# Two small transfers of an attention and phase-mixing kernel move from SyncE's queue to ScalarE's, and the first K follows the first Q directly

## The chip, the cores and the metric

The kernel runs on one core of a Trainium2 chip. The core has five engines with queues of their own: TensorE (PE, matrix products), VectorE (DVE), ScalarE (ACT), GpSimd (POOL) and SyncE (SP), which here does nothing but issue transfers. Transfers are carried out by 16 DMA engines that all queues share. The metric is the time of one execution on the device in microseconds; lower is better. The kernel before takes 221.73 us (median of three runs, 221.65 to 223.01).

## The reference

An attention block with polynomial features is followed by a token-mixing block whose input is the attention's output. Sizes: batch 4, 4 heads, 1088 tokens, head size 32, sketch size R = 8; the second block works on 128 columns.

```python
def phi(x):                                    # 32 -> 8 * 8 features
    a = einsum('rd,bhsd->bhsr', S1, x)
    b = einsum('rd,bhsd->bhsr', S2, x)
    return einsum('bhsi,bhsj->bhsij', a, b).reshape(..., 64)

q_p, k_p = phi(q), phi(k)
kv  = einsum('bhsf,bhsd->bhfd', k_p, v);  z = sum(k_p, axis=2)
num = einsum('bhsf,bhfd->bhsd', q_p, kv)
den = einsum('bhsf,bhf->bhs', q_p, z) + 1e-06
x   = (num / den), heads side by side          # (4, 1088, 128)

theta = x @ w_theta
yr = einsum('ts,bsd->btd', w_tok_r, x * cos(theta))
yi = einsum('ts,bsd->btd', w_tok_i, x * sin(theta))
u  = x + yr + yi
out = u + maximum(u @ w_ch, 0)
```

The weights and the sketch matrices S1, S2 come as 64-bit floating-point numbers, q, k and v as 32-bit ones.

## The kernel before

The kernel is written as a list of operations (`op`), each with its engine, the buffers that it reads and writes, and a function that emits its instructions. They are not emitted in the order of the text: `SEQUENCE` (L51) is a list of operation numbers written out by hand, and `Layout.issue` walks it. Each engine gets its instructions in that order and works them off strictly in that order; between engines there are semaphore waits where one reads what another wrote. `PLACES` gives each buffer a fixed slot in the on-chip memory.

`FILLS` (L127) adds empty matrix products (`spin`, L388) on TensorE in front of chosen operations: `(290, 1)` means one in front of operation 290. A positive count writes to a bank that nobody reads. A negative count, which the list of before doesn't use, writes into the bank that the operation itself is about to fill, for each new bank tile of that operation.

The work has three stages.

- Loading and features (about the first 57 us). For each of the four batches Q, K and V are loaded as 128 partitions by 1152 numbers (576 KB each, L661; some K a second time, L699). ScalarE squares a whole tensor and sums it (Q in L979, K in L683) so that a scale can be chosen; VectorE rounds the tensor to a half-precision part (`hf`, L338) and a rest; TensorE multiplies the parts (L354) and turns blocks (L1003 for Q, L780 for K). GpSimd issues accumulating transfers (L348) that add a rounded part to a second copy.
- The sketch matrices. S1 and S2 arrive in a small tile `st` by two transfers: L404 (`s_t`, 128 rows of 16 numbers, the matrix repeated for the four heads) and L405 (`s_2`, 8 rows of 32 numbers). Both write a tile that VectorE has cleared first (L411). `L418` on ScalarE is the first reader; it turns the 64-bit words into 32-bit numbers together with VectorE (L338, L341) and L430. The largest entry (`m2`, L460) goes over TensorE (L441) to a scale (L472), and the scaled matrices (L473, L474) feed the small products `psc`, `sbt`, `sbk` of GpSimd that the feature products need.
- Token mixing (the rest). The rows of the two 1088 x 1088 weight matrices are loaded (L614) and unpacked by ScalarE (L619, L621), and TensorE forms the products with a scheme that shares blocks between batches.

The order around the change, by engine, at the start. SyncE issues: Q of batch 0 (L661); the two small transfers (L404, L405); K of batches 0 to 3; Q of batches 1 and 2; the first rows of the token weights; and so on. ScalarE: the load of its function tables and a warm-up with the sine (L394), then L418, the square of Q0 (L979), of K0 (L683), L430, the square of K1, a scale of Q0 (L993), the square of K2, and L472 to L474. TensorE: 12 empty products, the turns of Q0, L441, a sum over partitions (`sm`,`ones`), 15 empty products (operation 64, which is one itself, and its fill of 14), and then the products of K0's rounded part (`hf`).

The planner's dependency rule is in `Layout.op`: each operation of ScalarE is made to depend on the first one (`leader`), the warm-up behind the table load. It adds edges to the planner's graph; the order that is emitted is the written list.

Of the kernel before, what the change touches and what calls it, by code (L numbers as in the profile page):

```python
# [48 lines left out]
QFIX = 2.006  # L49
NFIX = 1.002  # L50
SEQUENCE = (  # L51
# [74 lines left out]
)  # L126
FILLS = (  # L127
    (290, 1), (64, 14),
)


# [15 lines left out]
class Layout:  # L147
# [12 lines left out]
    def op(self, eng, dur, fn, w=(), r=(), acc=(), hold=(), lk=0, kind=0, mode=0, n=1, fly=0.0):  # L160
        o = Op()
        o.lk, o.fly, o.stage, o.kind, o.mode, o.n = lk, fly, self.stage, kind, mode, n
        o.i, o.eng, o.dur, o.fn = len(self.ops), eng, dur, fn
        o.succ, pred, o.bufs = [], set(), []
        if eng == "A":
            pred.update(self.leader)
            self.leader = self.leader or [o.i]

        def parts(x):
            return x if isinstance(x, tuple) else (x, None)  # L170

        def hits(table, b, key):
            t = table.get(b, {})
            return [v for k, v in t.items() if k is None or key is None or k == key or (
                isinstance(k, tuple) and k[0] == key) or (isinstance(key, tuple) and key[0] == k)]

        for x in r:
            b, key = parts(x)
            pred.update(hits(self.last_w, b, key))
            for s in hits(self.sums, b, key):  # L180
                pred.update(s)
            o.bufs.append(b)
        for x in list(w) + list(acc):
            b, key = parts(x)
            pred.update(hits(self.last_w, b, key))
            for s in hits(self.readers, b, key):
                pred.update(s)
            o.bufs.append(b)
        for x in w:
            b, key = parts(x)  # L190
            for s in hits(self.sums, b, key):
                pred.update(s)
        for x in r:
            b, key = parts(x)
            self.readers.setdefault(b, {}).setdefault(key, set()).add(o.i)
        for x in w:
            b, key = parts(x)
            if key is None:
                self.last_w[b] = {None: o.i}
                self.readers[b], self.sums[b] = {}, {}  # L200
            else:
                self.last_w.setdefault(b, {})[key] = o.i
                self.readers.setdefault(b, {})[key] = set()
                self.sums.setdefault(b, {})[key] = set()
        for x in acc:
            b, key = parts(x)
            self.sums.setdefault(b, {}).setdefault(key, set()).add(o.i)
        o.bufs = list(dict.fromkeys(o.bufs + list(hold)))
        for b in o.bufs:
            b.ops.append(o.i)  # L210
        pred.discard(o.i)
        o.pred = sorted(pred)
        for p in o.pred:
            self.ops[p].succ.append(o.i)
        self.ops.append(o)
        return o
# [53 lines left out]
def kernel(  # L270
# [12 lines left out]
    B, _, NC, H, D = q.shape  # L283
    S, DM = out.shape[1], out.shape[2]
    R = s_2.shape[0]
# [32 lines left out]
    pools = {c: maker(c, w) for c, (_, w) in classes.items()}  # L318
    L = Layout(classes)
    op, buf = L.op, L.buf  # L320

    def at(*name):
        L.stage = "".join(str(x) for x in name)

    V, A, G, T, SY = nc.vector, nc.scalar, nc.gpsimd, nc.tensor, nc.sync

    def fixed(shape, dt, name):
        b = Buf(None, shape, dt, name)
        n = math.prod(shape) * WORD[dt]
        b.ap = view(const.tile([P, (n + 3) // 4], F32, tag=name, name=name), shape, dt)  # L330
        return b

    def tt(eng, o, a, b, f):
        eng.tensor_tensor(out=o, in0=a, in1=b, op=f)  # L334

    def ts(o, a, s1, op0, s2=None, op1=None, eng=None):
        kw = {} if op1 is None else {"op1": op1}
        (eng or V).tensor_scalar(out=o, in0=a, scalar1=s1, scalar2=s2, op0=op0, **kw)  # L338

    def stt(o, a, s, b, op0, op1, eng=None):  # L340
        (eng or V).scalar_tensor_tensor(out=o, in0=a, scalar=s, in1=b, op0=op0, op1=op1)  # L341
# [4 lines left out]
    def join(n, dst, src, w, r):  # L346

        op("G", n * 2.55e-3, lambda: G.dma_start(dst(), src(), accum_op=ALU.add), w, r, kind=2)  # L348

    def vop(n, fn, w, r, two=False, lk=0):  # L350
        op("V", dve2(n) if two else dve(n), fn, w, r, lk=1 if two else lk)
# [4 lines left out]
    def bc(x, axis, shape):  # L356
        return x.unsqueeze(axis).to_broadcast(shape)
# [40 lines left out]
    NS = 2 * R + D  # L398
    sp = fixed((2, NS), F32, "sp")
    wide = s_t.dtype != F32  # L400

    def read_heads():
        dst = st() if wide else sp()[:, 0]
        SY.dma_start(dst[:, 0:2 * R], bc(s_t.rearrange("d t r -> d (t r)"), 0, [H, D, 2 * R]))  # L404
        SY.dma_start(dst[0:R, 2 * R:NS], s_2)  # L405

    if wide:
        st = fixed((NS,), I64, "st")
        y = fixed((NS,), I32, "sy")
        z = fixed((NS,), I32, "sz")  # L410
        op("V", 0.1, lambda: V.memset(st().bitcast(F32), 0.0), [st], [])  # L411
        op("S", 0.7, read_heads, [st], [], kind=1, n=2)

        def words():
            w = st().bitcast(I32).rearrange("p (n t) -> p n t", t=2)
            return w[:, :, 0], w[:, :, 1]

        op("A", 0.25, lambda: A.activation(sp()[:, 0], words()[1].bitcast(F32), AF.Prelu, scale=2.0**-112,  # L418
                                           alpha=-(2.0**32)), [(sp, 0)], [st])

        def unpack():
            wl = words()[0]
            x = sp()[:, 0].bitcast(I32)
            ts(x, x, 3, ALU.logical_shift_left)
            stt(x, wl, 29, x, ALU.logical_shift_right, ALU.bitwise_or)
            ts(y(), x, -(1 << 23), ALU.bitwise_and)
            ts(z(), wl, 0x1FFFFFFF, ALU.bitwise_and)

        op("V", 0.85, unpack, [(sp, 0), y, z], [st], lk=2)
        op("A", 0.25, lambda: A.activation(sp()[:, 1], z(), AF.Copy, scale=2.0**-52), [(sp, 1)], [z])  # L430
        vop(NS, lambda: tt(V, sp()[:, 1], sp()[:, 1], y().bitcast(F32), ALU.mult), [(sp, 1)], [y])
    else:
        op("V", 0.2, lambda: V.memset(sp(), 0.0), [sp], [])
        op("S", 0.7, read_heads, [sp], [], kind=1, n=2)

    def powers(mfn, m, n, name):

# [6 lines left out]
        def inv():  # L444
# [16 lines left out]
                                    op=ALU.max, apply_absolute_value=True), [m2], [(sp, 0)])  # L461
# [1241 lines left out]
```

## Time and profile before

The profile shows one execution. That execution took 222.03 us on the device; the instructions of the core span 220.3 us of it. Times of rows count from the start of the span.

| | before |
|---|---|
| median of three runs | 221.73 us |
| the profiled execution | 222.03 us |
| its span | 220.3 us |
| PE busy | 212.1 us (96%) |
| DVE busy | 188.1 us (85%) |
| ACT busy | 131.1 us (60%) |
| POOL busy | 80.7 us (37%) |
| mean granted clock of TensorE | 1.00 |

How to read the rows. The page cuts the span into 40 slices of 5.5 us; each digit of a strip is the busy share of a slice in tenths. A row of the timeline has the start, the duration, the engine, the line, the operation, the tile written and the tile read, a count, and in brackets the engine's idle time before it with what ended it; "SPq" is SyncE issuing a transfer, "PEld" the load of weights into TensorE. A row of the chain has start, duration, engine, tile and line. A row of the window view has the window, its length, busy time and count for PE, PEld, DVE, ACT and POOL, the granted clock, the mean busy share of the DMA engines, and GB/s moved.

### The profile page before, as it was taken

What the parts mean: (1) busy time and instruction counts of PE and PEld (TensorE: products, weight loads), DVE (VectorE), ACT (ScalarE), POOL (GpSimd) and SP (SyncE); (2) the same over time, 40 slices, a digit from 0 to 9 for tenths busy, and PEclk for the clock granted to TensorE, in tenths of its full rate; (3) what the DMA queues carried; (4) which work ended last, traced back from release to release, by engine and by line L of the source; (5) the groups of instructions that cost most, each with busy time, mean ns of one, the idle gap of its engine ahead of it and who ended that gap; (6) DMA issues with size and microseconds to landing.
All of it is one profiled execution on the core that took longest, in us unless ns stands there. A gap on an engine that the chain in (4) does not pass through costs nothing.

```text
span 220.3 us, 4200 instructions
## 1 busy us (share of the span) xinstructions
PE 212.1 (96%) x1481; PEld 177.1 (80%) x1481; DVE 188.1 (85%) x449; ACT 131.1 (60%) x277; POOL 80.7 (37%) x119
## 2 busy tenths in 40 slices
PE   7998999989999999999999999999999999999992
PEld 4697999976898796778888887888887888887882
DVE  2798999989999999999999999989999669567352
ACT  3896999979989899999989632662510100000000
POOL 1057934211013042064360746934360459251000
PEclk9999999999999999999999999999999999999999
DMA  6999999999759979987999999999998639688332
GB/s 207 407 415 409 349 354 389 358 419 376 233 171 285 296 239 226 316 210 124 190 261 176 276 192 189 189 183 189 185 134 124 96 46 149 93 122 112 61 56 53
DMA packets 34969, 48.78 MB, mean 221 GB/s; under 512 B 19204, under 2 KB 22276, under 8 KB 34820
## 3 DMA queue, kind: packets, MB, share of 16 engines
q0 software_dynamic: 10368, 18.21, 47.3%
q1 hardware_dynamic: 24580, 30.30, 40.8%
q8 instruction: 12, 0.20, 0.3%
q14 instruction: 9, 0.07, 0.1%
HBM read 28.07 MB, written 2.23 MB: 138 GB/s over the span
## 4 chain that ended last, share of the span: by engine, by line
PE 69%; DVE 18%; DMA 7%; issue 2%; ACT 2%; SPq 1%; ACTq 0%; DVEq 0%
PE ps L354 64%; DMA big<-hf 4%; DVE big L334 4%; DMA big<-k_l 3%; DVE g L334 3%; DVE big L338 2%; PE ps L1137 2%; DVE sm L341 2%; PE ps L1085 2%; DVE lv L334 1%; DVE sm L334 1%; DVE big L341 1%; ACT big L683 1%; DVE hf L338 1%; DVE zs L334 1%
## 5 line engine op out<-in xcount | busy, mean ns | idle before, releaser
L354 PE MATMUL ps<-big,zs 128*128 128x288 f32 (+3 forms) x450 | 107.3, 386 | 0.0
L354 PEld LDWEIGHTS ps<-big,zs 128*128 128x128 f32 x450 | 81.2, 190 | 18.4 <-DVE big L341 1.1
L348 POOL DMA_DIRECT2D big<-big x49 | 49.1, 1396 | 72.1 <-DVE big L338 24.0
L619 ACT ACTIVATE big<-zs 128x544 f32<-128x544 f32 x32 | 22.7, 721 | 1.8 <-DMA zs<-w_tok 1.8
L341 DVE SCALAR_TENSOR_TENSOR big<-ps,even,big 128x272 f32<-128x272 f32 (+3 forms) x34 | 16.1, 488 | 7.9 <-PE ps L354 7.8
L621 ACT ACTIVATE big<-zs 128x1088 int32<-128x1088 uint32 x16 | 19.6, 1225 | 0.7 <-DMA big<-big 0.5
L348 POOL DMA_DIRECT2D big<-hf x9 | 11.8, 1459 | 13.4 <-DVE big L334 6.9
L348 POOL DMA_DIRECT2D big<-g x10 | 9.8, 1112 | 18.4 <-DVE big L341 7.4
L1560 ACT ACTIVATE g<-ps,even 128x272 f32<-128x272 f32 x3 | 1.5, 488 | 22.4 <-PE ps L354 22.4
L354 PE MATMUL ps<-mf,big 128*128 128x96 f32 x72 | 14.4, 295 | 0.0
L338 DVE TENSOR_SCALAR big<-big 128x544 int32<-128x544 int32 (+1 forms) x33 | 14.0, 446 | 0.0
L1328 ACT COPY g<-ps 128x128 f32<-128x128 f32 x2 | 0.5, 266 | 21.8 <-PE ps L1326 21.8
L334 DVE TENSOR_TENSOR zs<-ps,g 128x768 f32<-128x768 f32 (+2 forms) x20 | 12.4, 630 | 1.0 <-issue 0.4
L354 PEld LDWEIGHTS <-hf 128*128 128x128 f16 (+1 forms) x144 | 12.2, 108 | 1.0 <-DVE hf L338 0.6
L341 DVE SCALAR_TENSOR_TENSOR big<-ps,big 128x288 f32<-128x288 f32 (+1 forms) x15 | 6.6, 438 | 7.4 <-PE ps L354 7.4
L354 PE MATMUL ps<-big,big 128*128 128x128 f32 x72 | 10.7, 280 | 1.1 <-DMA big<-hf 1.1
L334 DVE CUSTOM_DVE_ANT_0 big<-big,big 128x1088 uint16<-128x1088 uint16 x16 | 11.6, 729 | 0.1
L334 DVE TENSOR_TENSOR g<-lv 128x768 f32<-128x768 f32 x12 | 11.2, 954 | 0.3 <-PE ps L1137 0.2
L334 DVE TENSOR_TENSOR big<-big,hf 128x1152 f32<-128x1152 f32 x8 | 11.0, 1372 | 0.0
L354 PEld LDWEIGHTS ps<-mf,big 128*128 128x128 f32 x72 | 10.9, 191 | 0.0
L354 PE MATMUL ps<-w,big 128*128 128x128 f32 x76 | 10.5, 276 | 0.0
L354 PE MATMUL ps<-mv,hf 128*128 128x96 f16 x108 | 10.5, 206 | 0.0
(215 smaller groups left out, 442.6 us busy)
## 6 DMA issues: line engine op xcount, KB each, us to landing
zs<-w_tok SPq DMA_DIRECT2D x17, 1088.0 KB, 9.6
big<-big POOLq DMA_DIRECT2D x40, 272.0 KB, 7.3
big<-k_l SPq DMA_DIRECT2D x7, 576.0 KB, 6.6
big<-q_l SPq DMA_DIRECT2D x4, 576.0 KB, 8.8
big<-v_l SPq DMA_DIRECT2D x4, 576.0 KB, 11.3
big<-hf POOLq DMA_DIRECT2D x3, 576.0 KB, 9.3
big<-hf POOLq DMA_DIRECT2D x6, 272.0 KB, 6.4
big<-g POOLq DMA_DIRECT2D x10, 136.0 KB, 3.1
```

The source lines that it names most:

```text
L334: eng.tensor_tensor(out=o, in0=a, in1=b, op=f)
L338: (eng or V).tensor_scalar(out=o, in0=a, scalar1=s1, scalar2=s2, op0=op0, **kw)
L341: (eng or V).scalar_tensor_tensor(out=o, in0=a, scalar=s, in1=b, op0=op0, op1=op1)
L348: op("G", n * 2.55e-3, lambda: G.dma_start(dst(), src(), accum_op=ALU.add), w, r, kind=2)
L354: T.matmul(o, lhs, rhs, start=start, stop=stop, skip_group_check=True)
L619: op("A", 0.19 + HT * 0.0009, lambda j=j: A.activation(dst[j](), words()[1][:, j * HT:(j + 1) * HT].bitcast(F32), AF.Prelu, scale=scale, a ...
L621: op("A", 0.22 + S * 0.0009, lambda: A.activation(stp().rearrange("p r n -> p (r n)"), words()[0].bitcast(U32), AF.Copy, scale=2.0**-29), ...
L683: op("A", act(n) + 0.1, lambda: A.activation(flat(r()), kc(), AF.Square, accum_out=km()[:, 1:2]), [r, (km, 1)], [kx])
L1085: T.transpose(x()[:, i], xs()[:, off + i * P:off + (i + 1) * P], ident())
L1137: T.transpose(tr()[:, i * P:(i + 1) * P], qp()[:, i * H + 2 * n:i * H + 2 * n + 2].rearrange("p h i j -> p (h i j)"), ident())
L1328: op("A", act(P), lambda: A.copy(ot()[:, :P], tp()), [ot], [tp])
L1560: op("A", act(QT), lambda: A.mul(w(), to.out(0), evens[b]()[:, 5:6]) if b else A.copy(w(), to.out(0)), [w], [to.parts[0]] + ([evens[b]] if ...
```

## The change

`SEQUENCE` begins with Q0, the clearing of `st`, and the small transfers, which now belong to ScalarE. ScalarE's queue so begins with L404 and L405, followed by the table load; SyncE's begins with Q0 and K0. The small transfers are marked (`kind=3`) so that they aren't taken for ScalarE's leader. `FILLS` has one empty product less in front of operation 64 (so 14 in all ahead of the products of K0's rounded part), one in front of operation 28 (the product of `psc`), and two in front of operation 82 (the first product of `sbt`), the latter written into the banks that the operations fill.

```diff
 SEQUENCE = (
-    0, 1, 32, 290, 294, 5, 6, 31, 2, 4, 7, 292, ...
+    32, 5, 6, 0, 1, 290, 294, 31, 2, 4, 7, 292, ...
...
 FILLS = (
-    (290, 1), (64, 14),
+    (290, 1), (64, 13), (28, -1), (82, -2),
 )
...
-        if eng == "A":
+        if eng == "A" and kind != 3:
             pred.update(self.leader)
             self.leader = self.leader or [o.i]
...
     def read_heads():
         dst = st() if wide else sp()[:, 0]
-        SY.dma_start(dst[:, 0:2 * R], bc(s_t.rearrange("d t r -> d (t r)"), 0, [H, D, 2 * R]))
-        SY.dma_start(dst[0:R, 2 * R:NS], s_2)
+        A.dma_start(dst[:, 0:2 * R], bc(s_t.rearrange("d t r -> d (t r)"), 0, [H, D, 2 * R]))
+        A.dma_start(dst[0:R, 2 * R:NS], s_2)
...
-        op("S", 0.7, read_heads, [st], [], kind=1, n=2)
+        op("A", 0.7, read_heads, [st], [], kind=3, n=2)
```

The branch for 32-bit sketch matrices, which isn't taken here, gets the same edit.

More of the change, by code (lines that the diff above doesn't have):

```diff
@@ L433 @@
         op("V", 0.2, lambda: V.memset(sp(), 0.0), [sp], [])
-        op("S", 0.7, read_heads, [sp], [], kind=1, n=2)
+        op("A", 0.7, read_heads, [sp], [], kind=3, n=2)
     def powers(mfn, m, n, name):
```

2 rows, old and new, of the table SEQUENCE are left out of this document.

## The prediction

> **What bounds the kernel now.** I read the page first: its totals, the chain that ended last, and the strip of the memory engines.
>
> ```profile
> span 220.3 us, 4200 instructions
> PE 212.1 (96%) x1481; PEld 177.1 (80%) x1481; DVE 188.1 (85%) x449; ACT 131.1 (60%) x277; POOL 80.7 (37%) x119
> ...
> DMA  6999999999759979987999999999998639688332
> GB/s 207 407 415 409 349 354 389 358 419 376 233 171 285 296 239 226 316 210 124 190 261 176 276 192 189 189 183 189 185 134 124 96 46 149 93 122 112 61 56 53
> ```
>
> A slice is 5.5 us. PE is busy 96% of the span. The DMA engines are full from the second slice to the tenth (55 us) and move 350 to 420 GB/s there; the first slice shows 6 tenths and 207 GB/s. So the start is a loading stage with a hole in it. The chain in order of time says what hangs on that hole:
>
> ```profile
> 1.53 0.35 SPq L404
> 1.94 0.45 SPq L405
> 2.44 0.35 SPq L661
> 2.83 0.42 SPq L661
> 3.30 6.57 DMA big<-k_l
> ...
> 13.46 2.42 PE ps L354 x21
> ...
> 36.25 9.38 DMA big<-hf
> ...
> 57.34 7.49 PE ps L354 x95
> ```
>
> The chain begins with SyncE issuing the two small sketch transfers (L404, L405), then K. It follows a K transfer to 9.87, goes over ACT to PE at 13.46, over DVE to an accumulating transfer at 36.25, and from 57.34 on it is nearly all PE. There is no free time in it that a shift at the start could vanish into, except the two transfers. So the question is how much earlier the K that ends at 9.87 lands, and whether ACT is free for it.
>
> **The hole.** Half-microsecond windows; the last two columns are the DMA share and GB/s.
>
> ```profile
> 1.50:2.00 0.50, 0.50 (x3) 0.19 (x2) 0.26 (x5) 0.50 (x1) 0.12 (x1) 1.00 0.55 138
> 2.00:2.50 0.50, 0.50 (x3) 0.26 (x2) 0.20 (x5) 0.21 (x2) 0.00 (x0) 1.00 0.96 286
> 2.50:3.00 0.50, 0.50 (x3) 0.23 (x2) 0.00 (x0) 0.00 (x0) 0.00 (x0) 1.00 0.99 396
> 3.00:3.50 0.50, 0.50 (x3) 0.22 (x2) 0.00 (x0) 0.00 (x0) 0.00 (x0) 1.00 0.91 336
> 3.50:4.00 0.50, 0.50 (x3) 0.27 (x2) 0.00 (x0) 0.00 (x0) 0.00 (x0) 1.00 1.38 198
> 4.00:4.50 0.50, 0.50 (x3) 0.18 (x2) 0.00 (x0) 0.00 (x0) 0.00 (x0) 1.00 0.36 121
> 4.50:5.00 0.50, 0.50 (x3) 0.31 (x2) 0.00 (x0) 0.09 (x1) 0.00 (x0) 1.00 0.93 369
> 5.00:5.50 0.50, 0.50 (x6) 0.42 (x5) 0.28 (x2) 0.50 (x2) 0.00 (x0) 1.00 1.02 415
> ```
>
> Q (576 KB, 0.59 MB) is through by about 3.5: the four windows from 1.5 add up to 1156 GB/s times half a microsecond, 0.58 MB. Against 400 GB/s the four windows from 3.0 to 5.0 lack 64 + 202 + 279 + 31 = 576 GB/s times half a microsecond, 0.29 MB or 0.72 us of a full stream. Two things lie there: the 18 KB of small rows, and the first rows of K, whose issue at 2.44 comes too late to follow Q without a break.
>
> **The change, part by part.** SyncE's issues at the start:
>
> ```profile
> 0.72 0.39 SPq L661 DMA_DIRECT2D big<-q_l  x1
> 1.18 0.71 SPq L404 DMA_DIRECT2D st<-s_t  x1
> 1.94 0.45 SPq L405 DMA_DIRECT2D st<-s  x1
> 2.44 1.90 SPq L661 DMA_DIRECT2D big<-k_l  x4
> ```
>
> Then SyncE's own wait on VectorE, and the times from issue to landing of the transfers of K:
>
> ```profile
> SPq L404 <- DVE bdm L376: 0.4, 1, 0.4
> ...
> DMA to landing us min/median/max: 4.2/6.6/14.4
> ```
>
> And ScalarE:
>
> ```profile
> 0.72 1.28 ACT L394 ACT_TABLE_LOAD   x1 [0.72 <-PEq L1693]
> 2.01 0.20 ACT L394 ACTIVATE warm<-halfpi 128x1 f32<-128x1 f32 x1
> 4.91 0.25 ACT L418 ACTIVATE sp<-st 128x48 f32<-128x48 f32 x1 [2.69 <-DMA st<-s]
> ...
> 6.66 1.16 ACT L683 ACTIVATE big<-big 128x1152 f32<-128x1152 f32 x1 [0.36 <-DMA big<-k_l]
> ...
> 9.37 0.18 ACT L993 ACTIVATE qs<-sm 128x1 f32<-128x1 f32 x1
> 9.89 1.16 ACT L683 ACTIVATE big<-big 128x1152 f32<-128x1152 f32 x1 [0.34 <-DMA big<-k_l]
> ```
>
> SyncE loses two issues. K0 goes out where L404 began, at 1.18 in place of 2.44, and every later issue of SyncE moves up by 1.26 us until it meets its own waits for landings. The loads do not gain that much: Q's first bytes move in the window after 1.5, K0's would then be queued by about 2, before Q is through, and the engines cannot go faster than about 415 GB/s. What is gained is the hole, less what the small rows still cost. That cost has no row of its own; it lies between nothing and the 0.72. By their shapes (128 rows of 128 B, 8 of 256 B) they are 18 KB, which by bytes is 0.04 us of the 400 GB/s stream, and a share of 1.38 in one window says that many short packets overlapped; I take 0.1. The K stream so comes **0.6 us** earlier (ends 0 and, if the landing followed the issue, 1.26).
>
> *A rule weighed here.* The Trainium skill, DMA: Bandwidth & Descriptors, section "Issuing engines are not separate DMA queues", says that all issuers share the same 16 DMA engines and that a second issuer saves only issuing time, usually small beside the transfer. Taken alone it says 0 for the small transfers and speaks against the change; the windows from 3.5 to 4.5, with 198 and 121 GB/s, show that here the issuing time did open a hole.
>
> ScalarE gains two issues in front of its table load. L404 waited 0.4 for VectorE, which clears the same tile, until 1.53 by the chain; I let it wait as long on ScalarE, as nothing on VectorE moves. Then 0.35 and 0.45 with their gaps bring ACT to 2.40, the load (1.28) to 3.7 and the warm-up (0.20) to 3.9. L418 waits for the small rows anyhow, before until 4.91. So the load moves into idle time of 2.69 us and is late only if that cover goes. Behind L418 stand the squares of Q, K0 and K1 and, last before the chain's square of K at 9.89, L993, which ends at 9.55. From L418's start that is 4.64 us, of which 0.36 is the wait for K0, so 4.28 of work. The K of 9.89 lands at about 9.87 - 0.6 = 9.3. ACT is free for it if L418 starts by 9.3 - 4.28 = 5.0; the old 4.91 would do. The small rows are issued no later than before (1.94) and no longer stand behind Q in SyncE's queue: I take 3.9 to 4.9, and ACT costs nothing.
>
> *A second rule.* The Trainium skill, ScalarE: Activation LUTs, section "What ACT_TABLE_LOAD costs", adds a drain of about 1.38 us to the 1.28 us load. The trace shows none: the load ends at 2.00 and the warm-up starts at 2.01.
>
> TensorE: one empty product of L388 less ahead of K0's sums, one more ahead of the products of psc, two more ahead of those of sbt.
>
> ```profile
> 6.60 2.60 PE L388 MATMUL ps<-idle 128*128 128x384 bf16 x15
> 9.39 0.23 PE L354 MATMUL ps<-hf 128*128 128x128 bf16 x1 [0.19 <-DVE hf L338]
> ...
> 13.46 0.30 PEld L354 LDWEIGHTS ps<-sm,ones 128*128 128x128 f32 x2 [0.35 <-ACT big L683]
> ...
> 17.76 0.29 PEld L354 LDWEIGHTS ps<-psc,sx 8*128 8x128 f32 x2 [0.17 <-POOL sq L334]
> ...
> 18.42 0.35 DVE L341 SCALAR_TENSOR_TENSOR sm<-ps,kg,g 128x128 f32<-128x128 f32 x1 [0.35 <-PE ps L354]
> ...
> 19.70 0.60 PE L354 MATMUL ps<-sbt,sm 128*128 128x64 f32 x4 [0.45 <-POOL sbk L334]
> ```
>
> One costs 2.60 / 15 = 0.17 us. Without the one, K0's sums can start 0.19 + 0.17 = 0.36 earlier, at 9.03. PE then had 0.35 to spare at 13.46, where it waited for ACT, so PE alone allows 0.36 + 0.35 = 0.7: more than 0.6, and ACT stays the one that is late. The one before psc fills an idle of 0.17 exactly, the two before sbt 0.35 of 0.45. But each writes the bank that the real product then takes, so PE waits for its own product; that wait has no row. It costs nothing if it lies in those idle times, and at most about the work again, 3 x 0.17 = 0.5, if it adds to them. The psc products stand in front of a DVE step that waits for PE (18.42), so I take **0.1**. They could not gain anything: nothing real is issued earlier for them.
>
> The edit of the leader test and of the operation's kind changes no instruction; in the two builds the order on every engine is otherwise the same, POOL's queue included.
>
> From 13.46 to 57 everything is a chain of PE, DVE and one accumulating transfer in a stage where the engines are full. The same bytes go ahead of that transfer, and both its issue and the stream before it move up together. I carry the shift through at one for one. The sum: -0.6 + 0.1 = **-0.5 us**. The profiled execution took 222.03 (span 220.3), so 221.5 by its own time; that run lies 0.3 above the median of 221.73, and on the median the forecast is **221.2**.
>
> **The rivals.**
>
> 1. *Nothing arrives*: 221.7. Either the break before K0 is a start-up cost of any new transfer, or the gain is lost in the full stage up to 55 us, where the transfer of 9.38 us at 36.25 ends when the bytes before it are through. Against it: the next K transfers follow with no such hole (415 GB/s at 5.0). For it: 9.38 us is far from what 576 KB need at 400 GB/s (1.4 us), so other traffic sets its end. The rule on issuers above falls in with this.
>
> 2. *ScalarE becomes late* (slower). If the engines serve ScalarE's rows only after the queued Q and K0, L418 starts when K0 lands. K0 landed at 2.44 + 4.2 = 6.64 before and would at 6.0; then ACT is free at 6.0 + 4.28 = 10.3 against 9.89, 0.4 later, with the 0.1 of PE 0.5: **222.2**. It decides from L418 at 9.89 - 4.28 = 5.6. For a loss of 1% L418 would have to start at 7.8, after K1 too. Against it, 18 KB of rows; for it, Q and K0 are now issued ahead of them. A milder form is an idle of ACT behind its table load, now that the load ends late: up to 5.0 - 3.9 = 1.1 us of it costs nothing, 1.7 eats the whole gain, and the two rows of ACT, 2.00 and 2.01, speak against any. The drain that the Trainium skill gives in ScalarE: Activation LUTs, section "What ACT_TABLE_LOAD costs", would lie between the two, and the time by it at about 221.5.
>
> 3. *The whole issue time is won*: K lands 1.26 earlier, 1.16 after the 0.1, so 220.6. For it: K0's 4.2 us from issue to landing, counted from 1.18, end at 5.4. Against it: Q and K0 are 1.18 MB, and from 1.7 on at 400 GB/s they end at 4.7 before any landing delay; the later K stand in the same full stream.
>
> 4. *The shift meets another order downstream*: tiny POOL steps in the first 30 us take very different times beside DVE's work, and a new overlap could move the chain by a microsecond either way, at worst past 2.2 us.
>
> **How the numbers follow.** The forecast 0.50, rival 1 0.18, rival 2 0.13 (0.03 of it for the milder form), rival 3 0.07, rival 4 0.12. The range has to take in rivals 1 and 2 and most of rival 3, and the medians of three runs move by some tenths (221.65 to 223.01 were seen): 220.2 to 222.5. A difference of 1% (2.2 us) is about what a measurement of this kernel can tell from no change. The forecast and the first three rivals all lie within it; only rival 4, and rival 2 with L418 at 7.8, go beyond: faster 0.05, same 0.88, slower 0.07.
>
> **What the profile after would show.** The windows from 3.0 to 5.0 near 400 GB/s; SyncE's first K at about 1.2; two transfers of st on ScalarE's queue, its table load at about 2.4; L418 no later than 5.0; the square of K0 at about 6.1, the one of 9.89 at about 9.3; PE's 13.46 at 12.9; the chain's transfer of 36.25 at about 35.7 and its end near 45.1; the last PE stretch from about 56.8. The forecast is wrong if L418 starts after 5.6, if the hole stays though K is issued early, or if the shift seen at 13 us is gone at 57.

## The result: 2.7% slower

The changed kernel takes 228.04 us (median of four runs) against 222.12 for the kernel before, a ratio of 1.027 with a 95% interval of 1.021 to 1.033. A second set of four runs, further down, gave 1.018 (1.014 to 1.022). The profiled execution took 227.81 us, its span is 226.0, 5.7 more than the 220.3 of before.

The page of the changed kernel: span, the strips, the queue that is new, and the engines' shares of the chain (DMA 5%).

```profile
span 226.0 us, 4204 instructions
...
PEclk9769999999999999999999999999999999999998
DMA  6999699999937989999799899999999529788332
...
q10 hardware_dynamic: 148, 0.02, 0.1%
...
PE 78%; DVE 8%; DMA 5%; ACT 4%; POOL 2%; issue 1%; ACTq 0%
```

TensorE's granted clock, full throughout before, falls in the second and third slice (5.5 to 16.5 us). ScalarE's transfers have a DMA queue of their own, q10, with 148 packets. The same four half-microseconds as before, in the window view (the last columns are clock, DMA share and GB/s), and three later ones:

```profile
3.00:3.50 0.50, 0.50 (x3) 0.22 (x2) 0.00 (x0) 0.50 (x1) 0.00 (x0) 1.00 1.01 378
3.50:4.00 0.50, 0.50 (x3) 0.28 (x2) 0.00 (x0) 0.49 (x2) 0.00 (x0) 1.00 0.99 406
4.00:4.50 0.50, 0.50 (x3) 0.18 (x2) 0.00 (x0) 0.05 (x1) 0.00 (x0) 1.00 0.97 396
4.50:5.00 0.50, 0.50 (x3) 0.32 (x2) 0.00 (x0) 0.00 (x0) 0.00 (x0) 1.00 0.99 387
6.50:7.00 0.50, 0.00 (x0) 0.00 (x0) 0.00 (x0) 0.00 (x0) 0.00 (x0) 1.00 1.01 400
9.00:9.50 0.50, 0.00 (x0) 0.00 (x0) 0.00 (x0) 0.00 (x0) 0.00 (x0) 0.50 1.06 425
12.00:12.50 0.50, 0.50 (x3) 0.33 (x3) 0.00 (x0) 0.50 (x3) 0.00 (x0) 0.50 0.72 291
```

The hole is gone: 378, 406, 396 and 387 GB/s where there were 336, 198, 121 and 369. But at 6.5 and at 9 no compute engine does anything although the loads run at 400 GB/s, and by 9 the clock has fallen to half. The timeline says what they wait for; ACTq is ScalarE issuing a transfer.

```profile
0.98 1.15 ACTq L404 DMA_DIRECT2D st<-s_t  x1
...
1.17 2.01 SPq L661 DMA_DIRECT2D big<-k_l  x4
...
2.17 0.34 ACTq L405 DMA_DIRECT2D st<-s  x1
...
2.55 1.28 ACT L394 ACT_TABLE_LOAD   x1 [2.55 <-DVE grids L382]
...
3.85 0.20 ACT L394 ACTIVATE warm<-halfpi 128x1 f32<-128x1 f32 x1
...
10.73 0.24 ACT L418 ACTIVATE sp<-st 128x48 f32<-128x48 f32 x1 [6.68 <-DMA st<-s]
```

K0 is issued at 1.17, the table load ends at 3.83 and the warm-up follows at once, close to the forecast (1.2 and 3.7). What is late is the small rows themselves. They are issued by 2.51 and land at about 10.7, where L418 has waited 6.68 us for them. The chain in order of time goes through that landing:

```profile
2.17 8.47 DMA st<-s
...
10.73 0.25 ACT sp L418
...
11.88 0.37 PE ps L441
...
12.75 3.81 PE ps L388 x14
16.57 0.74 PE ps L354 x8
...
63.02 7.49 PE ps L354 x95
```

The row of 95 products that started at 57.34 before starts at 63.02. From there to the end of the span it is 163.0 us in both, so all of the loss lies ahead of it.

Where were the rows between 2.5 and 10.7? The page's queue table, asked for one microsecond at a time, from 5 to 10 (packets, MB, share of the 16 engines); before 5 it has no row for this queue:

```profile
q10 hardware_dynamic: 66, 0.01, 5.4%
...
q10 hardware_dynamic: 40, 0.01, 3.3%
...
q10 hardware_dynamic: 16, 0.00, 1.4%
...
q10 hardware_dynamic: 16, 0.00, 1.4%
...
q10 hardware_dynamic: 10, 0.00, 0.8%
```

Two things are in it. Nothing moves until 5, about where K0's rows end: by the start times of the packets, 258 large rows start first, as many as Q and K0 have (256) and two more, and the first small one starts at 5.06. Then the 148 packets need five microseconds to pass. They do not pass evenly: 57 go in the first half microsecond, and the last starts at 9.96. In the kernel before the same 18 KB passed on SyncE's queue between 3 and 4.5.

### The profile page after: what moved, and what is told of

Read it like the earlier page. It is cut to its first block, busy times and chain, and to the rows that moved or that the text cites. A ratio compares the mean times of both kernels' runs of the same rounds, so it can differ in the third digit from the quotient of the medians.

```text
span 226.0 us, 4204 instructions
## 1 busy us (share of the span) xinstructions
PE 214.0 (95%) x1483; PEld 178.1 (79%) x1483; DVE 187.6 (83%) x449; ACT 130.5 (58%) x277; POOL 79.5 (35%) x119
## 4 chain that ended last, share of the span: by engine, by line
PE 78%; DVE 8%; DMA 5%; ACT 4%; POOL 2%; issue 1%; ACTq 0%
PE ps L354 70%; DMA st<-s 4%; PE ps L388 2%; PE ps L1085 2%; PE ps L1137 1%; DVE big L338 1%; DVE g L334 1%; DVE big L334 1%; PE ps L1003 1%; PE ps L780 1%; DVE lv L334 1%; DMA out<-g 1%; ACT g L1141 1%; POOL sq L334 1%; POOL psc L572 1%
```

## The experiments

Two theories of the loss stood at the start. *Late rows*: L418 is late and everything that hangs on it, whichever queue carries the rows. *ScalarE's queue*: issuing there costs by itself (the late table load, a slow queue). A third, *empty products*, blamed the new fills.

**The rows late on SyncE's own queue.** The kernel of before, with four K issued ahead of the small transfers:

```diff
-    0, 1, 32, 290, 294, 5, 6, 31, 2, 4, 7, ...
+    0, 1, 32, 290, 294, 31, 36, 34, 35, 5, 6, 2, 4, 7, ...
```

> The kernel of before with one edit: SyncE issues all four K of the start ahead of the two small transfers, which stay on SyncE; no empty product is changed. Theory (late rows): the loss of the changed kernel comes from the late landing of the small rows alone (the first reader, L418, at 10.7 in place of 4.9), whichever queue carries them. Here they stand behind Q and four K, 5 x 576 KB at about 400 GB/s from 1.7 on, so they land at about 9.5 to 10 and L418 starts near 10, some 5 us late: 226 to 228 us, with TensorE idle from about 6.5 to 11 and its granted clock down for some microseconds. Rival (ScalarE's queue): the loss comes from issuing on ScalarE, its late table load or its own queue; then this kernel stays at 221.5 to 222.5 although L418 is late.

Measured: 228.54 us, a little above the range given, ratio 1.027 (1.021 to 1.033), the loss of the changed kernel without any transfer on ScalarE. Its ScalarE rows in the timeline:

```profile
2.01 0.20 ACT L394 ACTIVATE warm<-halfpi 128x1 f32<-128x1 f32 x1
10.78 0.24 ACT L418 ACTIVATE sp<-st 128x48 f32<-128x48 f32 x1 [8.57 <-DMA st<-s]
```

and the clock strip of its page:

```profile
PEclk9758999999999999999999999999999999999999
```

ScalarE was ready at 2.2 here and waited until 10.78. So the late landing is enough, and the late table load isn't needed for it.

**K0 held back until 2.2, the rows on ScalarE.**

```diff
-    32, 5, 6, 0, 1, 290, 294, 31, 2, 4, 7, 292, 3, 8, ...
+    32, 5, 6, 0, 1, 290, 294, 2, 4, 7, 292, 3, 31, 8, ...
...
+        def go():
+            if (nm, b) == ("k", 0):
+                V.memset(t()[:, 0, 0, 0:1], 0.0)
+            SY.dma_start(t()..., src[b]...)
```

> The changed kernel with K0's issue held back: VectorE clears one column of K0's tile after its constants (at about 2.2), so that SyncE can issue K0 only then, close to the 2.44 of before; the cleared column is overwritten by the load. The small transfers stay on ScalarE. Theory (late rows): without K0 queued behind Q the small rows meet only Q's rows and land by about 4 to 5, L418 starts no later than 5.2, TensorE is not idle at 7 to 11, the clock stays at 1.0: 221.5 to 222.8 us. Rival (ScalarE's queue): L418 stays beyond 8 us and the time at 226 to 228.

Measured: 222.83 us, ratio 0.9995 (0.995 to 1.004). The rows of ScalarE and TensorE, and the new queue from 3 to 7:

```profile
6.85 0.24 ACT L418 ACTIVATE sp<-st 128x48 f32<-128x48 f32 x1 [2.78 <-DMA st<-s]
...
11.32 0.23 PE L354 MATMUL ps<-hf 128*128 128x128 bf16 x1 [0.35 <-DVE hf L338]
```

```profile
q10 hardware_dynamic: 111, 0.01, 8.9%
...
q10 hardware_dynamic: 23, 0.00, 1.7%
...
q10 hardware_dynamic: 11, 0.00, 0.9%
...
q10 hardware_dynamic: 3, 0.00, 0.2%
```

The time is back, and the rows start moving right after 3, behind Q alone. But L418 is at 6.85, later than the 5.2 that was expected: the last packets still needed until 6.4, beside the K that follow. The last seven of them, from 5.3 on, start 0.18 to 0.19 us apart, and one large row of 4608 B takes 0.178 us: each waited for about one large row. And the run says a second thing that nobody expected: L418 and K0's first sum (11.32 against 9.39) are 1.9 us late and the time does not move, as far as its interval tells (0.4% up, 0.9 us). At the 95 products 0.85 us of the lateness is left (58.19 against 57.34).

**The fills**, once taken back in the changed kernel and once put alone into the kernel of before:

```diff
-    (290, 1), (64, 13), (28, -1), (82, -2),
+    (290, 1), (64, 14),
```

> The changed kernel with the empty products of before (15 ahead of K0's sums, none ahead of psc and sbt). Theory (late rows): the small rows still land at about 10.6; the four moved empty products are worth some tenths: 227 to 228.5 us. Rival (empty products): the new empty products, which wait for one another in the banks of real products, cost the time; then 221.5 to 223.

> The kernel of before with the empty products of the changed kernel and nothing else. The prediction took them at 0.1 us, with 0 and 0.5 as ends: 221.7 to 222.6 us. Rival (empty products): 225 or more.

Measured: alone they give 222.37 us, ratio 1.001 (0.997 to 1.005), no difference. Taken back from the changed kernel, 225.5 us in two runs, ratio 1.014 (1.007 to 1.020), less than was expected. L418 is at 9.50 in that profile, 10.73 in the first one of the changed kernel: how long the rows take varies from execution to execution. So the changed kernel was run again beside other kernels:

> The changed kernel once more, beside the two other kernels of this group on the same chip. 226.5 to 228.5 us, L418 between 9.5 and 10.8.

Measured: 226.44 us, ratio 1.018 (1.014 to 1.022), L418 at 8.96, both just under the ranges given. The two sets of the changed kernel differ by 0.9% (about 2 us), more than the 0.5 us that the prediction gave the fills at most, and what they are worth within it can't be said.

**The rows behind K0 on SyncE's queue.**

```diff
-    0, 1, 32, 290, 294, 5, 6, 31, 2, 4, 7, ...
+    0, 1, 32, 290, 294, 31, 5, 6, 2, 4, 7, ...
```

> The kernel of before with K0 ahead of the two small transfers on SyncE (Q, K0, s_t, s_2, further K); no empty product is changed. Queued behind Q and K0 on one ring, the small rows should land at about 5.5 to 6.5 and L418 start there, 1 to 1.5 us later than before. Theory A (one for one, as in the prediction): the square of K0 moves to about 7.3 and the time to 222.5 to 223.5. Theory B (slack): the first run with L418 at 6.85 took the time of before, so about 2 us of lateness of L418 are hidden behind the loads; then 221.5 to 222.5, the same as before.

Measured: 223.18 us, ratio 1.003 (1.000 to 1.007); L418 at 6.21. The time alone does not decide: 223.18 lies in theory A's range, and 1.3 us one for one would be a ratio of 1.006, inside the interval. The trace speaks for theory B: the 95 products start at 57.69, 0.35 later than before, and the span is 0.1 longer. The packets from 4.5 to 5.5 and from 5.5 to 6.5:

```profile
DMA packets 239, 0.36 MB, mean 364 GB/s; under 512 B 164, under 2 KB 164, under 8 KB 239
...
DMA packets 80, 0.35 MB, mean 346 GB/s; under 512 B 5, under 2 KB 5, under 8 KB 80
```

On one queue with the K all the small rows pass in one microsecond, at the place where ScalarE's needed five in the changed kernel.

**The second K held back until 4**, so that Q and K0 stand ahead of the rows as in the change, but nothing beside them:

```diff
-    ... 31, 2, 4, 7, ... 58, 36, 233, ...
+    ... 31, 2, 4, 36, 7, ... 58, 233, ...
...
+        def go():
+            if (nm, b) == ("k", 3):
+                A.copy(t()[:, 0, 0, 0:1], halfpi())
+            SY.dma_start(t()..., src[b]...)
```

> The changed kernel with its second K (batch 3) held back: ScalarE writes one column of that tile behind its warm-up, at about 4.0, so that SyncE issues this K and the next ones only then; the column is overwritten by the load. Q and K0 are issued as in the changed kernel, and the small rows still stand behind K0. Theory (two terms): the rows start where K0 ends, at about 5.0, and, as no other large rows are queued beside them, pass within about half a microsecond in place of 4 to 5; L418 starts at about 6 in place of 9.5 to 10.7, TensorE is idle for about 1 us only, the clock stays at 1.0, and by the slack seen so far the time is 221.5 to 223.5. Rival (ScalarE's queue is slow by itself): the rows take as long as before, L418 stays beyond 8 and the time at 225 or more.

Measured: 222.06 us, ratio 0.998 (0.996 to 1.000). ScalarE's queue in the microseconds from 4 to 6:

```profile
q10 hardware_dynamic: 82, 0.01, 6.7%
q10 hardware_dynamic: 66, 0.01, 5.3%
```

and L418 in the timeline:

```profile
5.90 0.24 ACT L418 ACTIVATE sp<-st 128x48 f32<-128x48 f32 x1 [1.76 <-DMA st<-s]
```

They start about where K0 ends (the first at 4.42) and are all through by 5.3. ScalarE's queue is not slow by itself; it is slow beside a backlog of large rows on SyncE's.

**The clock.** First with TensorE kept busy while it waits, then with the 13 empty products of the chain taken out:

```diff
-    (290, 1), (64, 13), (28, -1), (82, -2),
+    (290, 1), (12, 31), (64, 13), (28, -1), (82, -2),      # kept busy
+    (290, 1), (28, -1), (82, -2),                          # taken out
```

> The changed kernel with 31 more empty products ahead of the turn of m (L441), where TensorE is idle from 6.5 to 11.9 waiting for the small rows; 31 x 0.17 us is 5.3 us. Nothing else changes, L418 stays near 10.7. Theory (clock): the granted clock stays at 1.0, the 14 products ahead of K0's sums take 2.5 us in place of 3.8 and K0's first sum starts at about 15.4, where VectorE has the rounded part ready, in place of 16.5: about 1 us faster than the changed kernel, 226.5 to 227.5. Rival: the drop of the clock costs nothing here, 227.5 to 228.5.

> The changed kernel without the 13 empty products of the fill ahead of K0's sums (one, operation 64 itself, stays). In the changed kernel these products run at half clock from 12.6 to 16.2 and stand on the chain. Theory 1: they only delay; K0's sums start at 15.4 and the time falls by about 1 us to 226.5 to 227.5. Theory 2: they also bring the clock back; without them the sums of K0 run at half clock for some microseconds more and the time stays at 227.5 to 229.

Measured: 226.44 us (two runs, ratio 1.015, 1.009 to 1.021) and 226.42 us (two runs, 1.015, 1.009 to 1.021). Against the 228.04 and 226.44 of the changed kernel the medians decide nothing, since L418 moves from one execution to the next. Within a trace it can be read from L418 on. K0's first sum in the changed kernel, then with TensorE kept busy, then with the products taken out:

```profile
16.40 0.22 PE L354 MATMUL ps<-hf 128*128 128x128 bf16 x1
```

```profile
11.33 2.44 PE L388 MATMUL ps<-idle 128*128 128x384 bf16 x14
14.12 0.23 PE L354 MATMUL ps<-hf 128*128 128x128 bf16 x1 [0.35 <-DVE hf L338]
```

```profile
14.42 0.29 PE L354 MATMUL ps<-hf 128*128 128x128 bf16 x1 [2.31 <-DVE hf L338]
14.51 0.53 PE L354 MATMUL ps<-sm,ones 128*128 128x1 f32 x2
14.90 0.48 PE L354 MATMUL ps<-hf 128*128 128x128 bf16 x3
```

Kept busy, the 14 products take 2.44 us in place of the 3.8 in the chain of the changed kernel, and from L418 (9.54) to K0's first sum it is 4.58 us, near the 4.47 or 4.48 of the other kernels whose clock stayed full; in the changed kernel it is 16.40 - 10.73 = 5.67. Taken out, K0's first sum comes as early (4.67 after L418 at 9.75), but at half clock: three sums take 0.48, against 0.33 before. Its clock is back at full only at 19.1, the changed kernel's at 15.7. From L418 to the 95 products it is 53.48 us, against 52.29 and 52.82 in the two profiles of the changed kernel and 51.50 in the one kept busy. Both theories on the empty products hold a part: they stand on the chain, and they bring the clock back.

**One small transfer.** The host lays both matrices into one array, so that no clear and no wait is needed; the transfer is issued by SyncE between Q and K0 in the kernel of before, or by ScalarE first of all in the changed one:

```diff
+    small = np.zeros((P, 2 * r + D), S1.dtype)
+    small[:, :2 * r] = np.tile(np.stack([S1.T, S2.T], axis=1).reshape(D, 2 * r), (H, 1))
+    small[:r, 2 * r:] = S2
-        "s_t": bits(np.stack([S1.T, S2.T], axis=1)),
+        "s_t": bits(small),
...
-        A.dma_start(dst[:, 0:2 * R], bc(s_t.rearrange("d t r -> d (t r)"), 0, [H, D, 2 * R]))
-        A.dma_start(dst[0:R, 2 * R:NS], s_2)
+        A.dma_start(dst, s_t)
-        op("V", 0.1, lambda: V.memset(st().bitcast(F32), 0.0), [st], [])
+        op("V", 0.1, lambda: None, [st], [])
```

> The kernel of before with the two small transfers made one: the host lays both sketch matrices into one array of 128 rows of 48 numbers with zeros where the tile was cleared, so that VectorE's clear and the wait for it fall away and SyncE issues Q, one small transfer, K0. K0's issue moves from 2.44 to about 1.65, early enough to follow Q without a break, and the small rows stay ahead of K0 on the same ring. L418 starts at about 4.3, K0's square at about 6.1, the third K's square at about 9.3. Theory A (one for one): 0.6 us faster than before. Theory B (slack of the start): L418's path has slack, but the loads themselves are 0.6 us earlier, so 0 to 0.6 us faster. Either way no slower than before by more than 0.2.

Measured: 222.95 us, ratio 0.9995 (0.996 to 1.003), no difference. L418 was at 4.51 in its profile, but K0's square only at 8.36:

```profile
8.36 1.16 ACT L682 ACTIVATE big<-big 128x1152 f32<-128x1152 f32 x1 [2.46 <-DMA big<-k_l]
```

K0 was issued at 1.62 and took 6.7 us to land, so this kernel missed its point, and why K0 was slow there was not tried. The trace holds 16 completions of K0 (events that report a part as landed): the first came at 5.59, the last at 8.33, so that only a part of the transfer was slow (in the kernel before 5.72 to 6.64). TensorE then stood idle from 9.01 to 10.96, and its clock was at half from 12.0 to 15.4:

```profile
PEclk9969999999999999999999999999999999999999
```

> The changed kernel with the two small transfers made one (one array of 128 rows of 48 numbers, zeros where the tile was cleared, no clear and no wait), issued by ScalarE at about 0.7, beside Q and ahead of K0. Theory (two terms): the rows no longer stand behind K0, so they start at about 3.3; K0 follows Q without a break on SyncE's ring and the rows take turns with it, so they end between 4.5 and 6.5 and L418 starts at 5 to 7: no idle of 5 us, the clock at 1.0, and by the slack the time of before, 221 to 223. Rival (any use of ScalarE's queue costs): 225 or more.

Measured: 221.32 us, ratio **0.994 (0.992 to 0.997)**: faster than the kernel before and, beside it on the same chip, than the changed one (1.018). Its issue on ScalarE and the first reader, L417, in the timeline:

```profile
0.72 0.40 ACTq L404 DMA_DIRECT2D st<-s_t  x1
...
4.87 0.25 ACT L417 ACTIVATE sp<-st 128x48 f32<-128x48 f32 x1 [2.22 <-DMA st<-s_t]
```

its queue in the microseconds from 2 to 5:

```profile
q10 hardware_dynamic: 21, 0.01, 5.3%
q10 hardware_dynamic: 86, 0.03, 14.4%
q10 hardware_dynamic: 37, 0.01, 4.0%
```

and the stretch of 95 products in the chain in order of time:

```profile
56.44 7.49 PE ps L354 x95
```

Issued ahead of K0, the rows move beside Q and are through before 5; L417 (L418 before) is at 4.87, earlier than the 5 to 7 expected, and the time is better than "the time of before". K0 follows Q, and the stretch of 95 products starts 0.9 us earlier than in the kernel before.

This kernel differs from the changed one in a second way, and the two ways were not tried apart. Behind the issue of L404 the trace holds 4 completions in every kernel with two small transfers, and 16 for the single array. If each stands for one DMA engine (the trace names none), L404's 128 rows go through four of the sixteen, 32 on each, and the single array's through all, 8 on each. The single array, too, had a backlog beside it: Q, K0 and three more K were issued by 3.2. The two queues from 3.48 to 3.67:

```profile
q1 hardware_dynamic: 16, 0.07, 93.7%
q10 hardware_dynamic: 16, 0.01, 11.6%
```

One small row passes for each large one, 16 at a time; groups start at 3.30, 3.50 and 3.69. At 0.19 us a turn, 8 rows on an engine make 1.5 us and 32 make 6, an estimate from this spacing. The single array's rows took from 2.60 to 4.24; those of the changed kernel, some of which did not wait, 4.9 us. Being ahead of K0 was not enough where K0 was held: there the old two transfers, though issued later than here, still needed 3.1 us, and L418 was at 6.85.

All profiles together, in us: the first reader of the rows, K0's first sum, the stretch of 95 products, and the span.

| kernel | L418 | K0's first sum | 95 products | span |
|---|---|---|---|---|
| before | 4.91 | 9.39 | 57.34 | 220.3 |
| before, new fills | 5.32 | 9.80 | 57.07 | 220.5 |
| one transfer on ScalarE | 4.87 | 9.35 | 56.44 | 218.9 |
| one transfer on SyncE | 4.51 | 10.96 | 58.63 | 221.0 |
| second K held | 5.90 | 10.37 | 57.65 | 220.3 |
| rows behind K0 on SyncE | 6.21 | 10.69 | 57.69 | 220.4 |
| K0 held | 6.85 | 11.32 | 58.19 | 220.6 |
| changed, kept busy | 9.54 | 14.12 | 61.04 | 223.4 |
| changed, old fills | 9.50 | 15.29 | 61.46 | 224.4 |
| changed, fill taken out | 9.75 | 14.42 | 63.23 | 225.7 |
| changed, again | 8.96 | 15.12 | 61.78 | 224.8 |
| changed | 10.73 | 16.40 | 63.02 | 226.0 |
| rows behind four K on SyncE | 10.78 | 17.43 | 63.92 | 227.0 |

The loss of the changed kernel adds up from it: L418 is 5.8 us later; at half clock the way to K0's first sum is 1.2 longer; from there to the 95 products it is 1.3 shorter (46.62 against 47.95); nothing after. 5.8 + 1.2 - 1.3 = 5.7, the difference of the spans. That the 1.3 was waiting for loads in the start of before fits the waits of ScalarE for K there, and was not followed further.

## Why the prediction was wrong

It forecast 221.2 us; the second of its rivals came true, at many times its price.

- *The hole and its size*: right. The four windows went from 1024 to 1567 GB/s in sum, and K0 was issued at 1.17. The K that landed at 9.87 before landed at 9.10 by its last completion, 0.77 earlier where 0.6 was forecast; the late rows hid it. That this is worth something fits the one transfer on ScalarE, which keeps K0 there and has the rows on time: 0.6% faster than before. The "about 415 GB/s" that the engines were said not to pass is a little low: a half-microsecond window of before shows 442 (12.0 to 12.5).
- *The table load*: right. It ended at 3.83, the warm-up followed at 3.85, and L418 did not wait for it.
- *"The small rows are issued no later than before and no longer stand behind Q in SyncE's queue: I take 3.9 to 4.9, and ACT costs nothing"*: this is the step that failed. L418 started at 9.0 to 10.7. The rows did stand behind what SyncE had issued earlier, Q and K0, with the first packet after 5; and beside the K on SyncE's queue they were slower, not freer. The 0.1 us that the sum gave them was priced by bytes and for rows that run in one stream. The runs price both parts: behind K0 on SyncE's queue L418 is at 6.21, behind K0 on ScalarE's with no backlog at 5.90, behind K0 on ScalarE's with the backlog at 9.0 to 10.7. So standing behind K0 costs 1.0 to 1.3 us, and the backlog on the other queue another 3 to 5.
- *"L404 waited 0.4 for VectorE, which clears the same tile"*: not borne out, without effect on the result. The row names `bdm` L376; the clear of `st` (L411) was over at 0.95, before L404 began. The issue takes 0.71 in all three places on SyncE's queue: begun at 1.18, at 1.63 behind K0, and at 3.26 behind four K, where the profile lists no wait for it.
- *Rival 2* named the place, the mechanism of its first half and the sign. Its price was 0.5 us because it let the rows land with K0. It had 7.8 as the start of L418 from which 1% is lost, and thought that out of reach.
- *The clock* stood in no step. An idle of 5.4 us ahead of L441 took it to half, and that made the way from L418 to K0's first sum 1.2 us longer.
- *"I carry the shift through at one for one"*: wrong for small shifts. L418 may be 1.9 us late (K0 held) without a change in the time that the runs can tell (0.4% at most). By the prediction's own sum a loss began at 5.6; at 6.85 the runs show none yet.
- *The fills*: 0.1 was forecast; alone they gave 1.001 (0.997 to 1.005), which tells neither 0.1 nor the 0.5 of its upper end from nothing.
- *The rule on issuers* (the Trainium skill, DMA: Bandwidth & Descriptors, section "Issuing engines are not separate DMA queues") was weighed for whether the change could gain, and set aside. That the transfers of both issuers interleave is what the trace shows. The Trainium skill, DMA: Bandwidth & Descriptors, section "Queues, rings and completion order", says that each engine goes round-robin between the queues at packet granularity. The traces fit it in part. Where the small rows run beside the backlog, one passes for each large one, a turn of 0.18 to 0.19 us against the 0.178 us of a large row (the single array, and the last rows where K0 was held). But 57 of the changed kernel's 148 packets, and 118 in the run again, passed in the first half microsecond, and before 4.9 none took a turn with Q or K0. Why the rows were held back until then is open.

## What to carry to other kernels

A small transfer that many things wait for is best issued ahead of the large ones. Here a second queue didn't let it overtake what was issued earlier, and beside a backlog on the other queue its short rows took turns with large ones. When a move takes such a transfer out of a shared order, ask first what is in flight when it starts, and price the wait by rows, not by bytes; if the completions count engines, also by how many engines share the rows. And where TensorE waits, count the clock: an idle of some microseconds is paid a second time behind it.

## What the runs showed of the hardware that was not expected

- Transfers issued by ScalarE at 0.98 to 2.51 moved no byte until 5.06, with 1.18 MB issued by SyncE before them. With only Q issued before, they started at 3.32; issued together with Q, at 2.60.
- The 148 packets passed in 0.9 us when no other large load was queued beside them, and in 3.1 to 4.9 when several were; the single array's needed 1.6 beside a like backlog.
- An issue of L404 took 1.15 us on ScalarE's queue and 0.71 on SyncE's, there also with no wait in sight; the single array's issue took 0.40 to 0.42 on either. What makes the difference is open.
- After TensorE went idle at 6.46 in the changed kernel, the granted clock fell to 0.50 at 8.9 and was back at 1.00 at 15.7, 3.9 us after TensorE began again at 11.88. From the start of the idle to the fall it took between 2.0 us (the run again) and 5.3 us (old fills, where it came after TensorE had begun again). The half clock lasted 3.4, 6.8 or 10.2 us in the traces that show it. An idle of 1.95 us was enough once (the single transfer on SyncE), and idles of 1.16 and 1.32 us (second K held, K0 held) were not.
- One part of a load can lag: in the kernel with the single transfer on SyncE K0 needed 6.7 us to land, where it needed 4.2 and 4.6 in the kernels before and after. The cause is open.
